# Attention and two expert layers in one kernel: GpSimd's start put in program order, sink rows and second queries on another DMA queue

## The chip, the cores and the metric

One core of a Trainium2 chip. The metric is device time of one execution in microseconds, the median of several runs.

## The reference

Attention over 2 batches, 8 heads, 768 positions and 64 dimensions, with a window of 128 keys and 4 sink keys that every query sees, then two dense layers in a row on the 1536 resulting tokens:

```
keep = is_sink | in_window
scores = np.where(keep, scale * q @ k.T, -1e9)
a = softmax(scores)                       # per query
x = (a @ v) as [1536, 512]
h = x @ moe_w_in;  g = where(h >= 1, h, where(h <= -1, 0, (h + 1)**2 / 4));  x = g @ moe_w_out
h = x @ moe2_w_in; g = where(h > 0, h, exp(min(h, 0)) - 1);                  return g @ moe2_w_out
```

The weights and the two numbers `n_sink` and `window` arrive as 64-bit values and are turned into fp32 on the chip.

## The kernel before

Attention is cut into segments of 256 queries (two blocks of 128); each segment has four jobs, one for a pair of heads. A job has these stages: `st_T` transposes k and q on TensorE into a PSUM bank (`qkps`, L466), copies them to `qkT` (L470) and puts the sink keys beside them: GpSimd copies the first four keys of a batch to `sk` (L480) and `sk` into `qkT` (L481), and keeps the last key block of the segment for the next one (`kept`, L474 and L476). `st_S` makes the scores `S` (L506), VectorE adds the mask and takes the maximum (L510), ScalarE takes the exponential (L512), GpSimd collects the sink columns in `psn` (L515). `st_X` transposes the result (`tps`, L539; copied by ScalarE to `pt`, L541). `st_V` multiplies by v (`ops`, L564). When a segment's four jobs are done, `st_sink` adds the sinks' part: `xps` with the matrix `vs` (L597) and `rps` with the matrix of ones `one` (L601). Its result goes to `xh` and `xl` (L607, L608).

`vs` is built by `vsink` from the sink rows of v, `vraw`. In the first call it also makes two constant sets, `one` and `sel`, with memsets and selects on GpSimd (L362 to L376). `load_vsink` loads `vraw` for both batches on ScalarE's DMA queue (L350); `load` puts the queries of the first two jobs there too (L398) and everything else on SyncE's queue.

The dense layers walk over blocks of 512 tokens and 16 slices of the hidden dimension: `gemm1` makes `h` (L171), `gemm2` adds to `y` (L210), each with three fp32r products of a high and a low part. A weight unit is loaded into `st` (L106, L109; three buffers) and converted from 64-bit by ScalarE (`ca` L138, `F` L139) and VectorE (`ca` L142 and L143, `F` L145), then split into `wh` (L158) and `wl` (L160).

A scheduler sets the order on each engine by priorities, except inside `manual_schedule`, where the named engines (TensorE alone, L766 and L773) keep the program's order. `go` runs attention's stages: 20 of them, then the rest of the first token block, then the others between the steps of the dense layers. DMAs of both queues take eight semaphores in turn, so each waits for the landing of the eighth before it.

Of the kernel before, what the change touches and what calls it, by code (L numbers as in the profile page):

```python
# [7 lines left out]
F32 = mybir.dt.float32  # L8
F32R = mybir.dt.float32r
# [3 lines left out]
ALU = mybir.AluOpType  # L13
# [5 lines left out]
NSINK = 4  # L19
# [262 lines left out]
class Attn:  # L282
# [61 lines left out]

    def load_vsink(self):
        R = self.H * NSINK
        self.vraw, self.vs, self.sel = [], {}, None
        for b in range(self.B):
            raw = self.const.tile([R, 1, self.D], F32, tag=f"vraw{b}", name=f"vraw{b}")
            self.nc.scalar.dma_start(out=raw[:, 0, :], in_=self.v[b, :, 0:NSINK, :])  # L350
            self.vraw.append(raw)

    def vsink(self, b):

        if b in self.vs:
            return self.vs[b]
        nc, const, H, D = self.nc, self.const, self.H, self.D
        R = H * NSINK
        L = 3 * R + 2 * H
        if self.sel is None:  # L360

            self.one = const.tile([L, H, D], F32R, tag="one", name="one")  # L362
            one = const.tile([L, H], F32, tag="oneh", name="oneh")
            nc.gpsimd.memset(one, 0.0)
            for j in range(2):
                nc.gpsimd.affine_select(out=one[3 * R:], in_=one[3 * R:], pattern=[[-1, H]],
                                        compare_op=ALU.not_equal, fill=1.0, base=-j * H, channel_multiplier=1)
            nc.gpsimd.tensor_copy(self.one, one.unsqueeze(2).to_broadcast([L, H, D]))
            self.sel = const.tile([3 * R, H], F32, tag="sel", name="sel")
            nc.gpsimd.memset(self.sel, 1.0)  # L370
            for g in range(3):
                s = self.sel[g * R:(g + 1) * R]
                nc.gpsimd.affine_select(out=s, in_=s, pattern=[[-NSINK, H]], compare_op=ALU.is_ge, fill=0.0,
                                        base=0, channel_multiplier=1)
                nc.gpsimd.affine_select(out=s, in_=s, pattern=[[NSINK, H]], compare_op=ALU.is_ge, fill=0.0,
                                        base=NSINK - 1, channel_multiplier=-1)  # L376
        raw = self.vraw[b]
        part = const.tile([3 * R, 1, D], F32R, tag="vpart", name="vpart")
        nc.gpsimd.tensor_copy(part[0:R], raw)
        nc.gpsimd.tensor_copy(part[R:2 * R], raw)  # L380
        nc.gpsimd.tensor_tensor(out=part[2 * R:], in0=raw, in1=f32(part[0:R]), op=ALU.subtract)
        shape = [3 * R, H, D]
        self.vs[b] = const.tile([L, H, D], F32R, tag="vs", name="vs")
        nc.gpsimd.memset(f32(self.vs[b][3 * R:]), 0.0)
        nc.gpsimd.tensor_tensor(out=self.vs[b][0:3 * R], in0=f32(part).to_broadcast(shape),
                                in1=self.sel.unsqueeze(2).to_broadcast(shape), op=ALU.mult)
        return self.vs[b]

    def load(self, what, seg, pr):
        nc, D, nq = self.nc, self.D, self.nq  # L390
        b, q0 = seg[0], seg[1]
        k0 = max(q0 - 1, 0)
        nk = q0 + nq - k0
        src, r0, n = {"q": (self.q, q0, nq), "k": (self.k, q0, nq), "v": (self.v, k0, nk)}[what]
        t = self.ld_p.tile([128, n, 2, D], F32, tag=what + "n", name=what + "n")
        for j in range(2):

            (nc.scalar if what == "q" and (seg, pr) in self.jobs[:2] else nc.sync).dma_start(  # L398
                out=t[:, :, j, :],
                in_=src[b, 2 * pr + j, r0 * BLK:(r0 + n) * BLK, :].rearrange("(n p) d -> p n d", p=128))  # L400
        self.nat[what, seg, pr] = t
# [54 lines left out]
    def st_T(self, seg, pr, st):  # L456
# [15 lines left out]
            self.kept[pr] = self.const.tile([128, BLK], F32, tag=f"kept{pr}", name=f"kept{pr}")  # L472
        if lead:
            nc.gpsimd.tensor_copy(T[:, 0, 0:BLK], self.kept[pr])  # L474
        if q0 + nq < self.S // BLK:
            nc.gpsimd.tensor_copy(self.kept[pr], T[:, nq, 0:BLK])  # L476
        kT, qT = T[:, 1 - lead:1 + nq], T[:, 1 + nq:, 0:BLK]
        if first:
            self.sk[pr] = self.const.tile([128, 1, NSINK], F32, tag=f"sk{pr}", name=f"sk{pr}")
            nc.gpsimd.tensor_copy(self.sk[pr], kT[:, 0:1, 0:NSINK])  # L480
        nc.gpsimd.tensor_copy(kT[:, :, BLK:], self.sk[pr].to_broadcast([128, nq + lead, NSINK]))  # L481
        st["qk", pr] = qT, kT

    def st_S(self, seg, pr, st, n):
# [221 lines left out]
def attention_moe_moe(ctx, tc, q, k, v, n_sink, window, w_in, w_out, w2_in, w2_out, out):  # L706
# [21 lines left out]
    with ExitStack() as c2:  # L728
# [6 lines left out]
        attn = Attn(tc, c2, q, k, v, xts, idn, const, segs, nq=NQ)  # L735
        moe = Moe(tc, c2, ws, out, xts, (full, full), half)

        attn.load("q", *attn.jobs[1])
        attn.load_vsink()
        warm = const.tile([128, 1], F32, tag="warm", name="warm")  # L740
        nc.scalar.activation(warm, half, AF.Exp)

# [18 lines left out]
        attn.spare = [lambda shape, name, t=t: moe.y_ps.tile(shape, F32, tag=t, name=name) for t in ("y0", "y1", "y2", "y3")]  # L761
        attn.spare += [lambda shape, name: moe.h_ps.tile(shape, F32, tag="h", name=name)] * 2

        for what, j in (("k", 1), ("k", 2), ("q", 2), ("v", 0)):
            attn.load(what, *attn.jobs[j])
        with tc.manual_schedule(engines={mybir.EngineType.PE}):  # L766
            go(n=1)
            moe.load(1)
            attn.load("v", *attn.jobs[1])
            moe.load(3)  # L770
            go(n=19)
        flag = windowed(tc, const, prm)
        with tc.manual_schedule(engines={mybir.EngineType.PE}):  # L773
            go(upto=need[0])
        moe.behind = attn.first
        attn.spare = []
# [56 lines left out]
```

## Time and profile before

| | us |
|---|---|
| median of 3 runs (660.87 to 662.45) | 661.15 |
| the profiled execution | 662.93 |
| its span | 661.2 |
| TensorE busy | 638.8 |
| VectorE busy | 376.2 |
| ScalarE busy | 450.6 |
| GpSimd busy | 267.8 |

Busy time is summed over the whole span; what limits a stage is seen only in that stage's rows. A row of a timeline has start, duration, engine, line, operation, output and input, and in brackets how long the engine idled before it and what ended that.

### The profile page before, as it was taken

To read this page: it belongs to the slowest core of one execution; us is meant where nothing else is said; L and a number is where in the kernel's file an instruction comes from. 1 tells how busy PE (TensorE), PEld (TensorE's weight loads), DVE (VectorE), ACT (ScalarE), POOL (GpSimd) and SP (SyncE) were. 2 spreads that over 40 slices of the span, in tenths; PEclk is the share of its full clock that TensorE was granted. 3 is DMA by queue.
4 is the path that set the end of the run, shared out by engine and by line. 5 is a ranking of instruction groups with operands and counts; after the bars stand their busy time and mean duration, and the time that the engine had idled before them with its cause. 6 is when DMAs were issued, how large, how long until landed. Compare 5 with 4: busy or idle time off the path is not lost.

```text
span 661.2 us, 9257 instructions
## 1 busy us (share of the span) xinstructions
PE 638.8 (97%) x3090; PEld 500.5 (76%) x3090; DVE 376.2 (57%) x742; ACT 450.6 (68%) x913; POOL 267.8 (40%) x310
## 2 busy tenths in 40 slices
PE   5899999999999999999999999999999999999995
PEld 2666767766777767888878888888888888888884
DVE  2899989999435244224987878777432222322221
ACT  2998998997666666557768878776655555555542
POOL 4320113112125334443645655554544444444441
PEclk8998999999999999999999999999999999999999
DMA  6577454764200000000433332321010000100001
GB/s 172 126 186 203 126 170 135 207 198 143 56 13 13 13 0 1 1 0 1 159 118 105 99 105 90 109 93 50 0 64 1 0 1 0 64 0 1 1 0 69
DMA packets 66922, 47.91 MB, mean 72 GB/s; under 512 B 44848, under 2 KB 61232, under 8 KB 66864
## 3 DMA queue, kind: packets, MB, share of 16 engines
q1 hardware_dynamic: 65552, 46.94, 24.6%
q8 instruction: 26, 0.43, 0.3%
q10 hardware_dynamic: 1312, 0.28, 0.2%
q14 instruction: 32, 0.26, 0.1%
HBM read 44.06 MB, written 3.15 MB: 71 GB/s over the span
## 4 chain that ended last, share of the span: by engine, by line
PE 81%; DVE 7%; issue 4%; ACT 4%; DMA 2%; POOL 1%; POOLq 0%; SPq 0%; DVEq 0%; ACTq 0%
PE h L171 36%; PE y L210 35%; PE S L506 4%; PE ops L564 3%; PE tps L539 2%; DVE ca L143 2%; PE qkps L466 1%; DVE F L145 1%; DVE ca L142 1%; DVE wl L160 1%; ACT pt L541 1%; DMA st<-in_moe_w_in_dram 1%; DVE P L510 1%; ACT P L512 1%; PE y L267 1%
## 5 line engine op out<-in xcount | busy, mean ns | idle before, releaser
L160 POOL TENSOR_TENSOR wl<-F,wh 128x512 fp32r<-128x512 f32 x160 | 219.6, 1380 | 229.6 <-ACT wh L158 216.9
L158 ACT CAST wh<-F 128x512 fp32r<-128x512 f32 x192 | 117.5, 618 | 97.1 <-PE h L171 89.4
L171 PE MATMUL h<-xh,wh 128*128 128x512 f32 x384 | 154.3, 402 | 0.5 <-DVE g L180 0.5
L171 PE MATMUL h<-xh,wl 128*128 128x512 f32 x384 | 150.5, 392 | 0.0
L171 PE MATMUL h<-xl,wh 128*128 128x512 f32 x384 | 150.5, 392 | 0.0
L187 ACT CAST gh<-g 128x512 fp32r<-128x512 f32 x96 | 59.7, 621 | 62.1 <-DVE g L184 36.2
L188 DVE TENSOR_TENSOR gl<-g,gh 128x512 fp32r<-128x512 f32 x96 | 68.3, 712 | 49.0 <-ACT gh L187 48.7
L184 DVE SCALAR_TENSOR_TENSOR g<-g,h 128x512 f32<-128x512 f32 x48 | 33.0, 687 | 110.9 <-ACT g L183 110.9
L171 PEld LDWEIGHTS h<-xh,wh 128*128 128x128 f32 x384 | 72.4, 189 | 20.6 <-issue 5.3
L171 PEld LDWEIGHTS h<-xh,wl 128*128 128x128 f32 x384 | 72.3, 188 | 15.3
L171 PEld LDWEIGHTS h<-xl,wh 128*128 128x128 f32 x384 | 72.7, 189 | 14.2 <-DVE xl L608 0.4
L210 PE MATMUL y<-gh,wh 128*128 128x512 f32 x192 | 78.4, 408 | 0.0
L210 PE MATMUL y<-gh,wl 128*128 128x512 f32 x192 | 75.2, 391 | 0.0
L210 PE MATMUL y<-gl,wh 128*128 128x512 f32 x192 | 74.9, 390 | 0.0
L145 DVE CUSTOM_DVE_ANT_0 F<-ca,F 128x1024 uint16<-128x1024 uint16 x64 | 71.5, 1119 | 4.5 <-DVE ca L143 1.8
L210 PE MATMUL y<-wh,gh 128*128 128x512 f32 x184 | 71.6, 389 | 0.0
L210 PE MATMUL y<-wl,gh 128*128 128x512 f32 x184 | 71.6, 389 | 0.0
L210 PE MATMUL y<-wh,gl 128*128 128x512 f32 x184 | 71.6, 389 | 0.0
L180 DVE SCALAR_TENSOR_TENSOR g<-h,g 128x512 f32<-128x512 f32 x48 | 33.0, 687 | 45.2 <-ACT g L179 45.1
L512 ACT ACTIVATE P<-P,nb 128x260 f32<-128x260 f32 (+1 forms) x96 | 46.6, 491 | 15.5 <-DVE nb L510 13.4
L515 POOL COPY psn<-P 128x8 f32<-128x8 f32 x48 | 13.0, 271 | 89.8 <-ACT P L512 81.9
L510 DVE CUSTOM_DVE_ANT_0 P<-S,mask 128x260 f32<-128x260 f32 (+1 forms) x96 | 34.8, 401 | 24.1 <-PE S L506 23.5
(105 smaller groups left out, 912.3 us busy)
## 6 DMA issues: line engine op xcount, KB each, us to landing
st<-in_moe_w_in_dram SPq DMA_DIRECT2D x32, 512.0 KB, 3.9
st<-in_moe_w_out_dram SPq DMA_DIRECT2D x32, 512.0 KB, 3.8
kn<-in_k_dram SPq DMA_DIRECT2D x48, 64.0 KB, 2.3
vn<-in_v_dram SPq DMA_DIRECT2D x32, 96.0 KB, 2.4
out_dram<-o SPq DMA_DIRECT2D x12, 256.0 KB, 2.1
qn<-in_q_dram SPq DMA_DIRECT2D x44, 64.0 KB, 2.4
vn<-in_v_dram SPq DMA_DIRECT2D x16, 64.0 KB, 2.1
qn<-in_q_dram ACTq DMA_DIRECT2D x4, 64.0 KB, 3.0
```

Of the source, the lines that this page charges most:

```text
L145: nc.vector.tensor_tensor(out=r, in0=ai, in1=r, op=ALU.add)
L158: nc.scalar.copy(hi, src)
L160: (nc.vector if i < self.KF else nc.gpsimd).tensor_tensor(out=lo, in0=src, in1=f32(hi), op=ALU.subtract)
L171: nc.tensor.matmul(h, lhsT=w[:, k * 128:(k + 1) * 128], rhs=x[:, k, c0:c0 + n], start=(k == 0 and p == 0), stop=(k == self.KD - 1 and p == 2))
L180: nc.vector.scalar_tensor_tensor(out=g, in0=h, scalar=1.0, in1=g, op0=ALU.max, op1=ALU.min)
L184: nc.vector.scalar_tensor_tensor(out=g, in0=g, scalar=-1.0, in1=h, op0=ALU.add, op1=ALU.max)
L187: ac = nc.scalar.copy(gh, g)
L188: dv = nc.vector.tensor_tensor(out=gl, in0=g, in1=f32(gh), op=ALU.subtract)
L210: nc.tensor.matmul(self.y[c], lhsT=a, rhs=b, start=(first and p == 0), stop=(last and p == 2))
L506: nc.tensor.matmul(S[h], lhsT=qT[hs, n, :], rhs=kT[hs].rearrange("p j k -> p (j k)")[:, j0 * KW:j0 * KW + W], start=True, stop=True)
L510: dv = nc.vector.tensor_tensor_reduce(out=o, in0=S[h], in1=self.mask[ty], op0=ALU.add, op1=ALU.min, scale=-self.scale, scalar=3.0e38, accu ...
L512: ac = nc.scalar.activation(o, o, AF.Exp, bias=nb[:, n, h:h + 1], scale=-1.0, accum_out=sm[:, n, 2 * pr + h:2 * pr + h + 1])
```

## The change

The constant sets move from `vsink` into a function of their own, `sink_sets`, which is called ahead of the first stage. `vraw` is loaded on SyncE's queue, behind the first loads of k, q and v. Of the queries only those of the first job stay on ScalarE's queue; those of the second go on SyncE's, between the second and the third keys. In `st_T` the sink keys are copied before the kept block. GpSimd joins TensorE in the parts whose order is the program's, and `windowed`, which makes the flag for the general path, moves into one such part.

```diff
     def load_vsink(self):
-        self.vraw, self.vs, self.sel = [], {}, None
+        self.vraw, self.vs = [], {}
...
-            self.nc.scalar.dma_start(out=raw[:, 0, :], in_=self.v[b, :, 0:NSINK, :])
+            self.nc.sync.dma_start(out=raw[:, 0, :], in_=self.v[b, :, 0:NSINK, :])
             self.vraw.append(raw)
+
+    def sink_sets(self):
+        nc, const, H, D = self.nc, self.const, self.H, self.D
+        R = H * NSINK
+        L = 3 * R + 2 * H
+        self.one = const.tile([L, H, D], F32R, tag="one", name="one")
+        one = const.tile([L, H], F32, tag="oneh", name="oneh")
+        nc.gpsimd.memset(one, 0.0)
+        for j in range(2):
+            nc.gpsimd.affine_select(out=one[3 * R:], in_=one[3 * R:], pattern=[[-1, H]],
+                                    compare_op=ALU.not_equal, fill=1.0, base=-j * H, channel_multiplier=1)
+        nc.gpsimd.tensor_copy(self.one, one.unsqueeze(2).to_broadcast([L, H, D]))
+        self.sel = const.tile([3 * R, H], F32, tag="sel", name="sel")
+        nc.gpsimd.memset(self.sel, 1.0)
+        for g in range(3):
...
     def vsink(self, b):
-        if self.sel is None:
...
     def load(self, what, seg, pr):
-            (nc.scalar if what == "q" and (seg, pr) in self.jobs[:2] else nc.sync).dma_start(
+            (nc.scalar if what == "q" and (seg, pr) == self.jobs[0] else nc.sync).dma_start(
...
     def st_T(self, seg, pr, st):
             nc.gpsimd.tensor_copy(T[:, 0, 0:BLK], self.kept[pr])
-        if q0 + nq < self.S // BLK:
-            nc.gpsimd.tensor_copy(self.kept[pr], T[:, nq, 0:BLK])
...
         nc.gpsimd.tensor_copy(kT[:, :, BLK:], self.sk[pr].to_broadcast([128, nq + lead, NSINK]))
+        if q0 + nq < self.S // BLK:
+            nc.gpsimd.tensor_copy(self.kept[pr], T[:, nq, 0:BLK])
...
-        attn.load("q", *attn.jobs[1])
-        attn.load_vsink()
         warm = const.tile([128, 1], F32, tag="warm", name="warm")
...
-        for what, j in (("k", 1), ("k", 2), ("q", 2), ("v", 0)):
+        for what, j in (("k", 1), ("q", 1), ("k", 2), ("q", 2), ("v", 0)):
             attn.load(what, *attn.jobs[j])
-        with tc.manual_schedule(engines={mybir.EngineType.PE}):
+        attn.load_vsink()
+        attn.sink_sets()
+        with tc.manual_schedule(engines={mybir.EngineType.PE, mybir.EngineType.Pool}):
...
-        flag = windowed(tc, const, prm)
-        with tc.manual_schedule(engines={mybir.EngineType.PE}):
+            flag = windowed(tc, const, prm)
             go(upto=need[0])
```

How this moves instructions shows at three places. The first is GpSimd's queue from its constant sets to the sink keys of the first job (numbers behind a name tell buffers apart). Before:

```order
L379 CAST vpart<-vraw_134 32x64
L380 CAST vpart<-vraw_134 32x64
L366 AFFINE_SELECT oneh<-oneh 16x8
L373 AFFINE_SELECT sel<-sel 32x8 x3
L384 MEMSET vs 16x512
L366 AFFINE_SELECT oneh<-oneh 16x8
L375 AFFINE_SELECT sel<-sel 32x8 x3
L381 TENSOR_TENSOR vpart<-vraw_134,vpart 32x64
L368 CAST one<-oneh 112x512
L476 COPY kept_195<-qkT 128x128
L480 COPY sk_197<-qkT 128x4
L385 TENSOR_TENSOR vs<-vpart,sel 96x512
```

The same place in the changed kernel:

```order
L361 AFFINE_SELECT oneh<-oneh 16x8
L368 AFFINE_SELECT sel<-sel 32x8 x3
L361 AFFINE_SELECT oneh<-oneh 16x8
L370 AFFINE_SELECT sel<-sel 32x8 x3
L363 CAST one<-oneh 112x512
L481 COPY sk_214<-qkT 128x4
L482 COPY qkT<-sk_214 128x2x4
L484 COPY kept_213<-qkT 128x128
```

The steps on `vraw` and `vs` have left this place; they stand now behind the sink copies (`psn`) of the sixth job.

The second place is SyncE's DMA queue from its start, behind the load of `window`. Before:

```order
L398 DMA kn<-in_k_dram 128x2x64 x6
L398 DMA qn<-in_q_dram 128x2x64 x2
L398 DMA vn<-in_v_dram 128x2x64 x2
L106 DMA st<-in_moe_w_in_dram 128x4x256
L398 DMA vn<-in_v_dram 128x2x64 x2
L398 DMA kn<-in_k_dram 128x2x64 x2
L398 DMA qn<-in_q_dram 128x2x64 x2
L109 DMA st<-in_moe_w_out_dram 128x1024
L106 DMA st<-in_moe_w_in_dram 128x4x256
```

The same queue in the changed kernel:

```order
L401 DMA kn<-in_k_dram 128x2x64 x4
L401 DMA qn<-in_q_dram 128x2x64 x2
L401 DMA kn<-in_k_dram 128x2x64 x2
L401 DMA qn<-in_q_dram 128x2x64 x2
L401 DMA vn<-in_v_dram 128x2x64 x2
L350 DMA vraw_182<-in_v_dram 32x1x64
L350 DMA vraw_184<-in_v_dram 32x1x64
L106 DMA st<-in_moe_w_in_dram 128x4x256
L401 DMA kn<-in_k_dram 128x2x64 x2
L401 DMA qn<-in_q_dram 128x2x64 x2
L401 DMA vn<-in_v_dram 128x2x64 x2
L109 DMA st<-in_moe_w_out_dram 128x1024
```

Two query loads and two loads of `vraw` are new ahead of the first weights `st`; each keys or queries row of two is one job.

The third place is ScalarE from the exponentials of the third job to those of the fourth and the copy (`pt`) behind them. Before:

```order
L512 ACTIVATE P,sm<-P,nb 128x132 x2
L512 ACTIVATE P,sm<-P,nb 128x260 x2
L541 COPY pt<-tps 128x384 x2
L138 ACTIVATE ca<-st 128x512
L139 ACTIVATE F<-st 128x512
L512 ACTIVATE P,sm<-P,nb 128x132 x2
L512 ACTIVATE P,sm<-P,nb 128x260 x2
L541 COPY pt<-tps 128x384 x2
```

The same place in the changed kernel:

```order
L515 ACTIVATE P,sm<-P,nb 128x132 x2
L515 ACTIVATE P,sm<-P,nb 128x260 x2
L544 COPY pt<-tps 128x384 x2
L138 ACTIVATE ca<-st 128x512
L139 ACTIVATE F<-st 128x512
L138 ACTIVATE ca<-st 128x512
L139 ACTIVATE F<-st 128x512 x2
L138 ACTIVATE ca<-st 128x512
L158 CAST wh_926<-F 128x512
L515 ACTIVATE P,sm<-P,nb 128x132 x2
L515 ACTIVATE P,sm<-P,nb 128x260 x2
L544 COPY pt<-tps 128x384 x2
```

The conversions of the second and third weight units and the first `wh` now stand ahead of the fourth job's exponentials.

## Rows read from the trace of the kernel before

**Rows 1.** The page, part 1: busy us (share of the span) xinstructions by engine

```profile
PE 638.8 (97%) x3090; PEld 500.5 (76%) x3090; DVE 376.2 (57%) x742; ACT 450.6 (68%) x913; POOL 267.8 (40%) x310
```

**Rows 2.** Stretches: us, their length, busy us by engine, PE clock, DMA share, GB/s

```profile
10.00:20.00 10.00, 6.21 (x38) 4.21 (x38) 3.74 (x18) 4.18 (x17) 6.03 (x24) 0.66 0.92 244
...
24.00:58.00 34.00, 29.21 (x233) 21.34 (x229) 32.56 (x110) 33.28 (x97) 7.77 (x31) 1.00 0.68 174
...
83.00:110.00 27.00, 26.41 (x142) 19.55 (x137) 24.88 (x57) 24.23 (x54) 8.09 (x14) 1.00 0.54 159
```

**Rows 3.** Chain of waits, 0 to 30 us: start, us, what

```profile
2.01 6.15 issue
...
9.73 0.52 POOL vs L384
...
13.79 1.68 PE S L506 x8
```

**Rows 4.** Timeline of POOL, 0 to 24 us: start, us, instruction, idle before

```profile
8.18 0.23 POOL L379 CAST vpart<-vraw 32x64 fp32r<-32x64 f32 x1 [6.17 <-DMA vraw<-in_v_dram]
...
8.99 0.69 POOL L373 TENSOR_SCALAR_AFFINE_SELECT sel<-sel 32x8 f32<-32x8 f32 x3
...
11.64 0.61 POOL L368 CAST one<-oneh 112x512 fp32r<-112x512 f32 x1
...
12.57 1.03 POOL L385 TENSOR_TENSOR vs<-vpart,sel 96x512 fp32r<-96x512 f32 x1
```

**Rows 5.** Timeline of ACT and its DMA queue (ACTq), 0 to 24 us

```profile
1.28 3.98 ACTq L398 DMA_DIRECT2D qn<-in_q_dram  x4
5.40 2.05 ACTq L350 DMA_DIRECT2D vraw<-in_v_dram  x2
7.49 1.28 ACT L741 ACT_TABLE_LOAD   x1 [7.49 <-DMA qn<-in_q_dram]
...
8.89 1.05 ACT L470 COPY qkT<-qkps 128x512 f32<-128x512 f32 x2
```

**Rows 6.** Timeline of PE, 0 to 24 us

```profile
7.00 0.44 PE L466 MATMUL qkps<-idn,qn 128*128 128x128 f32 x2
...
19.30 0.93 PE L506 MATMUL S<-qkT 64*128 64x132 f32 x8
```

**Rows 7.** SP's DMA queue: timeline to 30 us; waits (us, times, longest)

```profile
8.37 0.47 SPq L106 DMA_DIRECT2D st<-in_moe_w_in_dram  x1
...
11.02 0.93 SPq L398 DMA_DIRECT2D qn<-in_q_dram  x2
...
SPq L398 <- DMA prm_i<-in_window_dram: 1.8, 1, 1.8
```

**Rows 8.** Single DMAs issued at 4.88, 11.48, 13.03, 11.99 us: KB, us to landing

```profile
qn<-in_q_dram ACTq DMA_DIRECT2D x1, 64.0 KB, 2.1
...
qn<-in_q_dram SPq DMA_DIRECT2D x1, 64.0 KB, 2.6
...
kn<-in_k_dram SPq DMA_DIRECT2D x1, 64.0 KB, 5.0
...
st<-in_moe_w_out_dram SPq DMA_DIRECT2D x1, 512.0 KB, 4.2
```

**Rows 9.** Timelines of DVE (first row) and of ACT (second), 0 to 24 us

```profile
7.63 0.50 DVE L343 TENSOR_SCALAR mask<-mask 128x260 f32<-128x260 f32 x2
...
22.95 0.67 ACT L138 ACTIVATE ca<-st 128x512 f32<-128x512 f32 x1
```

**Rows 10.** Timelines of POOL, PE, DVE and PE, 22 to 62 us

```profile
33.79 0.66 POOL L515 COPY psn<-P 128x8 f32<-128x8 f32 x1 [0.55 <-ACT P L512]
...
35.70 0.50 PE L597 MATMUL xps<-pst,vs 112*128 112x256 f32 x2
...
37.66 1.28 DVE L604 TENSOR_TENSOR xb<-xps,xb 128x512 f32<-128x512 f32 x2
...
58.00 0.73 PE L171 MATMUL h<-xh,wh 128*128 128x512 f32 x2
```

More of the change, by code (lines that the diff above doesn't have):

```diff
@@ L346, in load_vsink @@
         R = self.H * NSINK
-        self.vraw, self.vs, self.sel = [], {}, None
+        self.vraw, self.vs = [], {}
         for b in range(self.B):
             raw = self.const.tile([R, 1, self.D], F32, tag=f"vraw{b}", name=f"vraw{b}")
-            self.nc.scalar.dma_start(out=raw[:, 0, :], in_=self.v[b, :, 0:NSINK, :])
+            self.nc.sync.dma_start(out=raw[:, 0, :], in_=self.v[b, :, 0:NSINK, :])
             self.vraw.append(raw)
+    def sink_sets(self):
[12 more added lines that the diff above has]
+        for g in range(3):
+            s = self.sel[g * R:(g + 1) * R]
+            nc.gpsimd.affine_select(out=s, in_=s, pattern=[[-NSINK, H]], compare_op=ALU.is_ge, fill=0.0,
+                                    base=0, channel_multiplier=1)
+            nc.gpsimd.affine_select(out=s, in_=s, pattern=[[NSINK, H]], compare_op=ALU.is_ge, fill=0.0,
+                                    base=NSINK - 1, channel_multiplier=-1)
     def vsink(self, b):
@@ L359, in vsink @@
         L = 3 * R + 2 * H
-        if self.sel is None:
[L362 to L376, printed above, removed]
         raw = self.vraw[b]
```

## The prediction, made before the changed kernel ran

> **What bounds the kernel now.** I read the page first: TensorE (PE) is busy for 97% of the span [rows 1], so a change to GpSimd (POOL) can only pay where PE is not the limit. The table of stretches says where that is. Behind 58 us PE is the limit: from 83 to 110 us it is busy 26.41 of 27 us. From 24 to 58 us ScalarE (ACT) is busy 33.28 of 34 us and VectorE (DVE) 32.56; from 10 to 20 us nobody is the limit: ACT works 4.18 us, DVE 3.74 us, and PE's clock is 0.66 on average [rows 2]. So there are three stages: a start that waits, a stage of attention and weight conversion that ACT and DVE fill, and from the first `h` matmul at 58.00 us [rows 10] a stage that PE fills. What is won at the start counts if it reaches that first `h`.
>
> The chain of waits names the start: 6.15 us from 2.01 us on in which it finds no work, then POOL's steps one by one, then the first score matmuls `S` at 13.79 us [rows 3]. The timeline of POOL shows why. Its first cast of the sink rows waited 6.17 us for the load of `vraw`, and everything behind it in POOL's queue stood still: the selects that make `sel` and `oneh`, `one`, and at the end `sk`, the copy of the sink keys without which no `S` may start [rows 4]. The timeline of ACT shows a second thing: its queue issues four q loads (3.98 us) and two `vraw` loads (2.05 us) before the table load at 7.49 us, so the first `qkT` is copied out of PSUM only at 8.89 us, while PE had finished the transposes of the second job at about 7.44 us [rows 5, 6]. The DMA queue of SyncE (SP) shows a third: each DMA waits for the eighth before it, 1.8 us at the ninth [rows 7].
>
> **The change, part by part.**
>
> *POOL's sets and its order.* The eight selects and `one` no longer stand behind the load. Three selects took 0.69 us, so eight are about 1.9 us, with `one` at 0.61 us [rows 4] 2.5 us: from 2.0 us on they are over by 4.6 us, before any `qkT` exists. Cost nothing; the cover is the wait for k and q. The five steps that build `vs` (two casts of 0.23 us and a product of 1.03 us [rows 4], a memset of 0.52 us [rows 3], a short subtraction: about 2.4 us with the gaps) go behind the sixth job's sink copies.
>
> *ACT's queue.* Two q loads instead of six loads. The four took 3.98 us with a wait among them, so two end between 2.3 and 3.3 us; with 1.28 us of table load and the warming exp ACT is free by 4.8 us at the latest, and the first `qkT` copy (half of 1.05 us) follows PE's transposes, ending at 6.9 us [rows 5]. `sk` and its copy into `qkT` take 0.4 us: ready at 7.3 us.
>
> *The second q on SP.* PE's order puts the transposes of the second job ahead of the first `S`. Its q is now the ninth DMA and waits for the parameter load, as the ninth did at 4.5 us; one that was issued at 4.88 us on ACT landed 2.1 us later [rows 8]. On SP the two go out at 4.9 and 5.4 us, land at 7.0 and 7.5 us, and with 0.44 us of transposes [rows 6] the first `S` starts at about 7.8 us instead of 13.79 us. **Lead: 6.0 us.** DVE then does the last two mask steps (0.50 us [rows 9]) behind the first mask-and-max, where they used to be covered: 0.5 us off.
>
> *SP's queue.* This is where I expect most of the lead to go. Ahead of the fourth k and q now stand the second q (two DMAs) and `vraw` (two) besides what stood there. Two q loads take 0.93 us on SP [rows 7], so k2, q2 and v0 take it from 5.8 to 8.6 us. `vraw` has no row on SP: on ACT the two took 2.05 us [rows 5], while other loads take 0.46 us each, so 0.9 to 2.05 us; I take 2.0, the row of the same load. Then `st` (0.47), k3 and q3: the last q3 DMA goes out at 12.5 us instead of 11.5 us. Before, it landed 2.6 us after issue, and the following k load, beside two weight loads, needed 5.0 us [rows 8]. I take 2.6: landed at 15.1 us. PE's order needs these transposes ahead of the third job's `S`, which so starts at 15.4 us instead of 19.30 us [rows 6]: **lead 3.9 us**, and the 0.5 us of the masks lies inside that wait. By the bounds (`vraw` at 0.46 us each; landing in 5.0 us) the lead is 5.0 or 1.5 us. Less idle could also spare PE the half clock at which its first eight `S` took 1.68 us against 0.93 us later [rows 3, 6]; but PE idles again before q3 lands, so I count nothing.
>
> The Trainium skill ("DMA: Bandwidth & Descriptors", section "Issuing engines are not separate DMA queues") says that issuing from several engines saves only the sequencer's time, usually small against the DMA. ACT's rows differ: there six issues held up the copies until 7.49 us. By the rule `vraw` would cost SP next to nothing, the lead would be 5.0 us and the time about 657.1 us.
>
> *ACT and DVE to the first `h`.* In the new order ACT converts three weight units and casts one `wh` in a row before the exps of the fourth job, where it did one unit. At about 0.6 us a conversion [rows 9] the surplus is some 2.9 us of work done earlier, not added. It starts 3.9 us earlier, at 19.1 us instead of 22.95 us [rows 9]. The third unit's weights are the eighth DMA behind the first unit's and wait for them: out at 10.6 us, landed 4.2 us later [rows 8] at 14.8 us, so the third unit's land at about 19.5 us. They are wanted four conversions behind 19.1 us, at 21.5 us, so I count no wait. Up to the last `xh` of the first token block, ACT's order holds one conversion step more than before (7 `ca` against 6): **0.6 us off**. DVE's holds one `ca` step and one `wl` more; it idles 1.44 us in that stage [rows 2], which takes them.
>
> *`vs` late.* `vs` now starts behind the sink copies of the sixth job, which ended at 34.45 us; 2.4 us later is 36.9 us on before's scale, where the `xps` matmuls ran at 35.70 us [rows 10]. PE would wait up to 1.2 us there; but DVE took the result only at 37.66 us [rows 10], behind other work. So 0 to 1.2 us; I take 0.4: **0.4 us off**.
>
> Everything else (kept keys behind sink keys; the flag inside the hand-ordered part) is off the path.
>
> **Sum.** 3.9 - 0.6 - 0.4 = 2.9 us earlier at the first `h`, 55.1 us instead of 58.00. From there PE has the same matmuls left and hardly idles, so the end moves with it. The profiled span is 661.2 us (that execution took 662.93 us); the median of the runs is 661.15 us. 661.15 - 2.9 = **658.2 us**.
>
> **Rivals.**
>
> 1. *The DMAs don't hold it.* `vraw` costs SP 0.46 us each, q3 lands in time, and ACT and DVE carry 5 to 6 us of lead on: 661.15 - 5.5 = 655.7 us. For it: DMAs of 64 KB landed in 2.1 us when the queue was short [rows 8]. Against it: SP's queue is longer by four DMAs, and the first unit's weights go out at 10.6 us instead of 8.37 us [rows 7].
>
> 2. *SP's queue takes nearly all of it.* q3 needs 5.0 us to land beside the weights: lead 1.5 us, less 1.0 us: 660.6 us, within what the measurement of this kernel can tell from no change (0.3%, 2.0 us: 659.2 to 663.1). For it: the row of 5.0 us [rows 8]. Against: at its issue only one weight load is in flight.
>
> 3. *Slower: ACT stands at the third unit's weights.* ACT works in order, and the exps of the fourth job now stand behind that conversion. The weights are issued only after the first unit's have landed. Until 21.5 us they cost nothing; each us beyond comes off the lead, and with 2.9 us to lose and 2.0 us to be seen it decides from a landing at 26.4 us on, 6.9 us later than I work out. With 27.0 us the time is 661.15 + 5.5 - 2.9 = 663.8 us. For it: SP's queue runs late by four DMAs. Against: two landings of 4.2 us one behind the other [rows 8] leave 2 us to spare.
>
> 4. *It does nothing for the end.* The lead reaches the first `h`, but the new mix of conversions and attention behind it lets PE wait as long: 661 us. For it: PE's order changes from the first `h` on. Against: PE idles 0.6 us in 83 to 110 us [rows 2], so there is little to re-mix, and conversions are further ahead.
>
> **How the numbers follow.** Forecast 0.44, rival 1 0.20, rival 2 0.24, rival 3 0.06, rival 4 0.06. The forecast's own spread is 656.6 to 659.6 us, nearly all of it below 659.2 us. Faster by over 0.3%: 0.41 of the forecast, 0.20 of rival 1 and a little of rival 2: 0.62. Within 0.3%: the rest of the forecast, of rival 2 and rival 4: 0.32. Slower: 0.06. The range goes from rival 1 with some room (655.0) to rival 2 with some room (661.1); what lies outside is rival 3, part of rival 4 and a lead above 6 us, under 0.2 in all.
>
> **What would show it.** In the changed kernel's trace: POOL without a wait for `vraw` ahead of `sk`; the table load before 4 us; first `S` near 7.8 us; third job's `S` near 15.4 us with PE waiting for a q load; conversions of three units in a row on ACT from about 19 us without a DMA wait; first `h` near 55 us; and the same distance from there to the end, 603 us. I am wrong if the third job's `S` does not wait for a DMA (rival 1), if it starts after 17 us (rival 2), if ACT waits on `st` before the fourth job's exps (rival 3), or if the stretch behind the first `h` changes by more than 1.5 us.

## The result and the profile after

The changed kernel takes 667.11 us (median of 5 runs, 665.92 to 668.61); the kernel before takes 661.15 us (660.73 to 662.45, 5 runs beside them). The ratio is 1.0088, with a 95% interval from 1.0067 to 1.0108: **slower by 6.0 us**, where I had forecast 2.9 us faster. The profiled execution of the changed kernel took 668.61 us, at the upper end of its runs; its span is 666.9 us, against 661.2 us before. Executions of one kernel differ here by up to 4.5 us, and the mean granted clock of PE differs between them, too (0.987 in the profiled execution of the changed kernel, 0.992 in the median one), so I take sizes from medians and places from traces.

PE's own work did not grow: it has the same 3090 instructions as in [rows 1], and they take 5.1 us longer.

```profile
PE 643.9 (97%) x3090; PEld 502.1 (75%) x3090; DVE 377.4 (57%) x742; ACT 451.7 (68%) x913; POOL 267.6 (40%) x310
```

The stretches of [rows 2] in the changed kernel (us, length, busy us by engine, PE clock, DMA share, GB/s):

```profile
10.00:20.00 10.00, 7.20 (x41) 4.14 (x40) 5.25 (x26) 6.33 (x26) 2.31 (x14) 0.71 0.84 228
24.00:58.00 34.00, 28.56 (x220) 21.14 (x218) 31.31 (x110) 29.95 (x87) 11.03 (x38) 0.95 0.65 162
83.00:110.00 27.00, 27.00 (x144) 19.38 (x143) 24.65 (x54) 24.63 (x52) 7.28 (x12) 1.00 0.49 146
```

From 24 to 58 us ACT and DVE now idle 4.05 and 2.69 us, where they idled 0.72 and 1.44 us before, and PE's clock is no longer 1.00 throughout. The stage that two engines filled now has holes. The chain of waits names other things at the start than in [rows 3]: the warm-up matmuls instead of GpSimd, and then a k load (start, us, what):

```profile
1.56 5.49 PE warmup L748 x6
11.57 3.55 DMA kn<-in_k_dram
```

PE's timeline shows where the lead goes (start, us, instructions; in brackets the idle time before and what ended it):

```profile
8.89 0.93 PE L509 MATMUL S<-qkT 64*128 64x132 f32 x8 [0.28 <-POOL qkT L482]
15.25 0.66 PE L469 MATMUL qkps<-idn,kn 128*128 128x128 f32 x2 [2.80 <-DMA kn<-in_k_dram]
16.41 1.68 PE L509 MATMUL S<-qkT 64*128 64x132 f32 x8
21.58 0.93 PE L509 MATMUL S<-qkT 64*128 64x132 f32 x8
25.04 0.44 PE L469 MATMUL qkps<-idn,kn 128*128 128x128 f32 x2 [0.92 <-DVE qkT L473]
27.77 1.24 PE L567 MATMUL ops<-pt,vn 128*64 128x256 f32 x8 [0.91 <-ACT pt L544]
34.72 0.59 PE L587 MATMUL sps<-idn,psn 128*48 128x128 f32 x2 [2.59 <-DVE psn L584]
35.10 1.92 PE L542 MATMUL tps<-idn,P 128*128 128x128 f32 x8
39.01 0.51 PE L600 MATMUL xps<-pst,vs 112*128 112x256 f32 x2
60.70 0.73 PE L171 MATMUL h<-xh,wh 128*128 128x512 f32 x2 [0.28 <-ACT xh L610]
```

The same row of `sps` in the kernel before:

```profile
33.00 0.38 PE L584 MATMUL sps<-idn,psn 128*48 128x128 f32 x2 [1.49 <-DVE psn L581]
```

The first `S` is 4.9 us earlier than before, the third job's 2.9 us earlier [rows 6], the fourth job's only 1.0 us (21.58 against 22.62 us). Then the lead turns: the sink transposes `sps` are 1.7 us late, the `xps` matmuls 3.3 us, the first `h` 2.7 us [rows 10].

Two kinds of loss stand in these rows. One is **the clock**: behind the wait of 2.80 us the third job's eight `S` take 1.68 us, where the first eight took 0.93 us. The granted clock is 0.50 there, the 1.2 GHz level, and 0.59 from 34 to 38 us, behind the wait of 2.59 us (stretches, columns as above):

```profile
16.00:20.00 4.00, 4.00 (x21) 2.29 (x21) 2.39 (x10) 1.98 (x8) 0.95 (x6) 0.50 1.04 309
34.00:38.00 4.00, 3.28 (x16) 2.93 (x18) 2.25 (x6) 2.56 (x6) 3.73 (x7) 0.59 0.44 100
```

The other is **the order** on ACT and DVE. ACT's timeline:

```profile
2.30 1.28 ACT L742 ACT_TABLE_LOAD   x1 [2.30 <-issue]
17.69 0.40 ACT L515 ACTIVATE P<-P,nb 128x132 f32<-128x132 f32 x1 [3.04 <-DVE nb L513]
21.50 0.67 ACT L138 ACTIVATE ca<-st 128x512 f32<-128x512 f32 x1
...
24.98 0.60 ACT L158 CAST wh<-F 128x512 fp32r<-128x512 f32 x1
25.49 0.40 ACT L515 ACTIVATE P<-P,nb 128x132 f32<-128x132 f32 x1
```

From 21.50 us on stand six conversion steps and a cast, three units' worth, ahead of the fourth job's exps at 25.49 us. Before, one unit stood there and these exps began at 24.11 us, although the job's `S` came 1.0 us later. DVE's timeline of the same stretch and of the sink chain:

```profile
22.20 0.43 DVE L142 TENSOR_SCALAR ca<-ca 128x512 int32<-128x512 int32 x1 [2.17 <-ACT ca L138]
...
24.90 0.28 DVE L513 CUSTOM_DVE_ANT_0 P<-S,mask 128x132 f32<-128x132 f32 x1
...
33.03 0.24 DVE L582 RECIPROCAL sm<-sm 128x16 f32<-128x16 f32 x1
33.19 0.62 DVE L143 SCALAR_TENSOR_TENSOR ca<-st,ca 128x512 int32<-128x512 int32 x1
33.73 0.16 DVE L583 CAST psn<-sm 128x16 fp32r<-128x16 f32 x1
33.81 0.68 DVE L160 TENSOR_TENSOR wl<-F,wh 128x512 fp32r<-128x512 f32 x1
34.41 0.16 DVE L584 TENSOR_TENSOR psn<-sm,psn 128x16 f32<-128x16 f32 x1
34.49 0.68 DVE L145 CUSTOM_DVE_ANT_0 F<-ca,F 128x1024 uint16<-128x1024 uint16 x1
35.10 0.72 DVE L160 TENSOR_TENSOR wl<-F,wh 128x512 fp32r<-128x512 f32 x1
```

DVE, too, idles 2.17 us and then does four conversion steps, while the `S` of the fourth job, there from 21.58 us on, waits until 24.90 us for its mask-and-max. And a `wl` step of 0.68 us stands inside the sink chain on which PE waits. SP's queue:

```profile
8.88 1.61 SPq L350 DMA_DIRECT2D vraw<-in_v_dram  x2
12.13 0.93 SPq L401 DMA_DIRECT2D qn<-in_q_dram  x2
15.17 0.96 SPq L401 DMA_DIRECT2D kn<-in_k_dram  x2
```

The load issued last here is the fifth job's k. Its two DMAs (KB, us to landing):

```profile
kn<-in_k_dram SPq DMA_DIRECT2D x2, 64.0 KB, 5.0
```

Before, it was issued at 13.03 us and also needed 5.0 us [rows 8]; now it lands 2.1 us later, at 20.2 to 20.7 us, and PE transposes it from 20.82 us on.

GpSimd did what the change says (`one` over at 4.7 us, then free). In the sink chain its casts for `vs` ran slowly:

```profile
4.07 0.61 POOL L363 CAST one<-oneh 112x512 fp32r<-112x512 f32 x1
8.40 0.19 POOL L481 COPY sk<-qkT 128x4 f32<-128x4 f32 x1 [3.71 <-ACT qkT L473]
34.48 0.79 POOL L382 CAST vpart<-vraw 32x64 fp32r<-32x64 f32 x1
35.32 0.58 POOL L383 CAST vpart<-vraw 32x64 fp32r<-32x64 f32 x1
```

The two casts, which took 0.23 us each ([rows 4] shows the first), take 0.79 and 0.58 us here, beside DVE's `F` and `wl` steps. The Trainium skill ("SBUF — State Buffer", section "Summary: rules for kernel authors") says that of a DVE step with two SBUF inputs and a GpSimd step that reads SBUF the second to issue is blocked until the first ends. The second cast agrees: it starts within DVE's `wl` step, which goes from 35.10 to 35.82 us, and ends just behind it, at 35.90 us. For the first cast the rows don't tell which of the two was issued first (34.48 and 34.49 us).

### The profile page after: what moved, and what is told of

Same layout as the page of the kernel before. It is cut to its first block, busy times and chain, and to the rows that moved or that the text cites. A ratio compares the mean times of both kernels' runs of the same rounds, so it can differ in the third digit from the quotient of the medians.

```text
span 666.9 us, 9253 instructions
## 1 busy us (share of the span) xinstructions
PE 643.9 (97%) x3090; PEld 502.1 (75%) x3090; DVE 377.4 (57%) x742; ACT 451.7 (68%) x913; POOL 267.6 (40%) x310
## 4 chain that ended last, share of the span: by engine, by line
PE 81%; ACT 6%; DVE 6%; issue 3%; DMA 2%; POOL 0%; POOLq 0%; SPq 0%; DVEq 0%; ACTq 0%
PE h L171 36%; PE y L210 34%; PE S L509 3%; PE tps L542 2%; PE ops L567 2%; ACT P L515 1%; DVE ca L143 1%; PE qkps L469 1%; DVE ca L142 1%; PE warmup L748 1%; ACT pt L544 1%; ACT ca L138 1%; DMA st<-in_moe_w_out_dram 1%; ACT wh L158 1%; PE y L267 1%
## 5 line engine op out<-in xcount | busy, mean ns | idle before, releaser
L518 POOL COPY psn<-P 128x8 f32<-128x8 f32 x48 | 12.5, 260 | 95.0 <-ACT P L515 87.1
L143 DVE SCALAR_TENSOR_TENSOR ca<-st,ca 128x512 int32<-128x512 int32 x64 | 45.9, 721 | 1.1
```

Source lines behind the costliest of these rows:

```text
L143: nc.vector.scalar_tensor_tensor(out=ai, in0=w1, scalar=-0x80000000, in1=ai, op0=ALU.bitwise_and, op1=ALU.bitwise_or)
```

## The experiments

**Theory at the start**: the lead of the start is real, and it is lost through the order of ACT and DVE, which is not written by hand and came out differently once the loads were moved, and through PE's idling. **Rival A**: SP's longer queue is the loss. **Rival B**: GpSimd's program order is, with `vs` made late. The median of the kernel before was 661.1 to 661.3 us beside all of these runs. The table has the starts of stages on PE in each trace (us) and the median of the runs (us).

| kernel | first S | third S | fourth S | sps | xps | first h | median |
|---|---|---|---|---|---|---|---|
| before | 13.79 | 19.30 | 22.62 | 33.00 | 35.70 | 58.00 | 661.15 |
| after | 8.89 | 16.41 | 21.58 | 34.72 | 39.01 | 60.70 | 667.11 |
| e1 GpSimd part alone | 10.02 | 15.20 | 19.23 | 29.62 | 33.53 | 55.40 | 659.80 |
| e2 moved loads alone | 11.95 | 18.35 | 21.70 | 34.70 | 39.02 | 60.62 | 665.06 |
| e3 after, vraw later on SP | 8.27 | 14.79 | 21.36 | 32.30 | 36.63 | 58.31 | 665.83 |
| e4 after, order held | 8.48 | 16.16 | 21.70 | 31.67 | 36.95 | 59.42 | 665.31 |
| e5 e1, vs early | 10.00 | 15.08 | 19.54 | 29.94 | 32.64 | 56.87 | 660.44 |
| e6 e4, vs early | 8.33 | 16.17 | 22.18 | 31.65 | 35.50 | 56.48 | 662.61 |
| e7 after, wl held | 8.62 | 16.17 | 21.77 | 33.30 | 37.62 | 58.55 | 664.48 |
| e8 after, vs early | 9.01 | 16.75 | 21.94 | 35.06 | 39.30 | 61.02 | 667.84 |
| e9 e6, fifth k first | 8.32 | 16.60 | 21.79 | 32.27 | 36.01 | 57.55 | 662.97 |
| e10 e6, vraw on ACT | 8.58 | 15.14 | 20.24 | 32.08 | 34.77 | 56.28 | 660.80 |
| e11 e1, vraw behind the exp | 8.82 | 14.84 | 19.92 | 31.75 | 35.41 | 56.70 | 660.17 |
| e12 e1, fifth k first | 9.95 | 15.09 | 18.41 | 28.97 | 32.63 | 53.86 | 659.29 |
| e13 e12, vs early | 10.00 | 14.76 | 18.22 | 29.66 | 32.36 | 54.03 | 658.69 |
| e14 e13, vraw behind the exp | 8.83 | 15.07 | 19.03 | 29.73 | 32.42 | 54.12 | 659.02 |

### The two halves of the change

**e1, GpSimd's part alone.** The changed kernel with its loads and flag put back:

```diff
-            (nc.scalar if what == "q" and (seg, pr) == self.jobs[0] else nc.sync).dma_start(
+            (nc.scalar if what == "q" and (seg, pr) in self.jobs[:2] else nc.sync).dma_start(
...
-            self.nc.sync.dma_start(out=raw[:, 0, :], in_=self.v[b, :, 0:NSINK, :])
+            self.nc.scalar.dma_start(out=raw[:, 0, :], in_=self.v[b, :, 0:NSINK, :])
...
+        attn.load("q", *attn.jobs[1])
+        attn.load_vsink()
         warm = const.tile([128, 1], F32, tag="warm", name="warm")
```

> The kernel before with the GpSimd part of the change alone: constant sets first, GpSimd in the program's order, sink keys ahead of kept keys. The second q and vraw stay on ACT's queue, so SP's queue is the old one, and PE's order is that of the kernel before (ACT's and DVE's but for a handful of places). Theory (what costs is the new order of ACT's and DVE's work that came with the moved loads, and PE's idling; GpSimd's part is good): first S at about 10.3 us instead of 13.79 (ACT is still held by its six issues until its table load at 7.49 us), 3 us of it reach the first h, 657 to 659 us. Rival A (the moved loads alone, by the longer SP queue): the same 657 to 659 us. Rival B (GpSimd's program order is what costs: vs is made late, and its steps are slow beside DVE): first h no earlier than 58.0, 661 to 665 us.

659.80 us (657.41 to 660.40), ratio 0.9970 (0.9957 to 0.9982): **faster**, though 0.8 us above the range of the theory, and rival B falls. The trace shows the wait for `vs` that I had put at 0.4 us:

```profile
10.02 0.94 PE L509 MATMUL S<-qkT 64*128 64x132 f32 x8 [2.70 <-POOL qkT L482]
33.53 0.51 PE L600 MATMUL xps<-pst,vs 112*128 112x256 f32 x2 [1.14 <-POOL vs L388]
```

**e2, the moved loads alone**, on the kernel before (the same lines the other way round; GpSimd as before).

> The kernel before with the moved loads alone (second q and vraw on SP); GpSimd as before, so that it still waits for vraw ahead of the sink copies. Theory: ACT and DVE get the new order (three units converted in a row behind the third job's exps) and the first S comes only with vraw at 12 to 13 us: 664 to 669 us, slower than before. Rival A: SP's queue costs the same here: 664 to 669 us. Rival B: without GpSimd's order there is no loss: 658 to 662 us.

665.06 us (662.50 to 665.42), ratio 1.0043 (1.0027 to 1.0059): **slower**, as expected. ACT's instructions stand in the changed kernel's order up to 42.9 us, and PE has its waits, so the new order came with the loads, not with GpSimd's part:

```profile
25.55 0.44 PE L466 MATMUL qkps<-idn,kn 128*128 128x128 f32 x2 [1.31 <-DVE qkT L470]
28.29 1.23 PE L564 MATMUL ops<-pt,vn 128*64 128x256 f32 x8 [0.91 <-ACT pt L541]
34.70 0.38 PE L584 MATMUL sps<-idn,psn 128*48 128x128 f32 x2 [2.05 <-DVE psn L581]
```

**e3, the same order with another queue**: on SP the two `vraw` loads go behind the fourth k and q.

```diff
-        attn.load_vsink()
         attn.sink_sets()
...
             attn.load("v", *attn.jobs[1])
+            attn.load_vsink()
             moe.load(3)
```

> The changed kernel with the two vraw loads moved on SP behind the first weight load, the fourth k and q and the second v. The order of PE, ACT, DVE and GpSimd is that of the changed kernel, only SP's differs: the last q DMA that PE waits for goes out about 1.6 us earlier. Theory (order, not queue): that wait shrinks from 2.8 to about 1.2 us, 0.5 to 1 us of it is left at the first h, 665.5 to 667 us. Rival A (SP's longer queue and the wait on it are the cause): 658 to 662 us. Rival B: no change, 667 us.

665.83 us (663.48 to 667.76), ratio 1.0075 (1.0062 to 1.0089): 1.3 us less than the changed kernel, as the theory said, but the two intervals overlap, so that rival B isn't excluded. (Its profiled execution was the fastest of its runs.) The fourth k now lands in time for a third `S` at 14.79 us, but the fourth `S` comes at 21.36 us, hardly earlier than in the changed kernel: `vraw` still stands ahead of the fifth k. Behind the fourth `S` this trace loses little, although its order is the changed kernel's on PE, ACT, DVE and GpSimd. ACT's timeline has the same conversions, begun 2.4 us earlier:

```profile
19.11 0.67 ACT L138 ACTIVATE ca<-st 128x512 f32<-128x512 f32 x1
23.08 0.41 ACT L515 ACTIVATE P<-P,nb 128x132 f32<-128x132 f32 x1
```

The fourth job's exps follow 1.72 us behind its `S`, against 3.91 us in the changed kernel, and `sps` 10.9 us behind it, against 13.1 us (10.4 us before). So, by these two traces, what this order costs depends on how late the third job is when ACT comes to the conversions.

### The order

**e4, order held.** The second to fourth conversion each stand behind the exps of one job more, and the first two `wl` steps behind `psn`:

```diff
-        if n == nq - 1 and (seg, pr) == self.jobs[2]:
-            self.first = (ac.ins, dv.ins)
+        if n == nq - 1 and (seg, pr) in self.jobs[2:7]:
+            self.first = (self.first or []) + [(ac.ins, dv.ins)]
...
-        after = self.behind if self.n_cv <= 4 else self.own ...
+        after = self.behind and self.behind[(0, 1, 2, 2)[self.n_cv - 1]] if self.n_cv <= 4 else self.own ...
...
+        with self.tc.issue_after(self.psn) if self.psn and i < 2 else nullcontext():
-        (nc.vector if i < self.KF else nc.gpsimd).tensor_tensor(out=lo, ...
+            (nc.vector if i < self.KF else nc.gpsimd).tensor_tensor(out=lo, ...
```

> The changed kernel with the order held: the second, third and fourth weight conversion each stand behind the exps of one attention job more (fourth, fifth, fifth job instead of all behind the third), and the first two wl steps behind the two psn steps of DVE. Loads and GpSimd as in the changed kernel. Theory: the lead of the start (4.9 us at the first S, 2.9 us at the third job's) stays, first h at 55.5 to 57.5 us, 658 to 661 us. Rival A (queue): the wait for the fourth q is still there, 665 to 668 us. Rival B (GpSimd's order): 665 to 668 us.

665.31 us (664.10 to 665.86), ratio 1.0055 (1.0042 to 1.0068): a miss for the theory, inside the range of both rivals. `sps` did move 3.1 us forward, to 31.67 us, but the next thing was late, `vs` on GpSimd, whose product ended at 36.90 us (the profile names `nb`, which was done long before):

```profile
36.95 0.80 PE L603 MATMUL xps<-pst,vs 112*128 112x256 f32 x2 [2.49 <-DVE nb L514]
```

**e6, order held and vs early**: GpSimd builds `vs` between the third and the fourth job.

```diff
-            go(n=19)
+            go(n=6)
+            attn.vsink(0)
+            go(n=13)
```

> The changed kernel with the order of conversions and of wl held, and vs built earlier on GpSimd as well. With the order held alone PE waited 2.49 us at the first xps matmuls until vs was there at 36.9 us, and ran the next 3 us at half clock. Theory: with vs early the wait is bounded by pst (35.4 us), no half clock behind it, first h 1.5 to 2.5 us earlier than with the order held alone, 662 to 664 us. Rival (the moved loads cost whatever the order): 665 us as before.

662.61 us (660.95 to 663.48), ratio 1.0018 (1.0009 to 1.0027): as expected. **e8** is the control, `vs` early without the order held.

> The changed kernel with vs built earlier on GpSimd, nothing else; the order of PE, ACT, DVE and SP is that of the changed kernel. In the changed kernel vs was there at 37.94 us and the xps matmuls ran at 39.01 us behind the score matmuls. Theory (there the sink chain of DVE and the half clock are the limit, not vs): 666.5 to 667.5 us, no change. Rival (GpSimd's late vs is the loss): 661 to 665 us.

667.84 us (665.75 to 668.14): 0.3 us above the range, but no change, as expected. In the changed kernel `vs` was late behind something later still. So holding the order is worth 667.84 - 662.61 = 5.2 us where `vs` is early, and 667.11 - 665.31 = 1.8 us where it is not (there the two intervals touch). In the traces of e8 and e6 4.5 us of the 5.2 us are there at the first `h` (61.02 against 56.48 us); behind it the two also differ in PE's order.

**e7, wl alone held**: only the last two lines of the diff of e4.

> The changed kernel with one order alone mended: the first two wl steps of DVE stand behind the two psn steps of the first segment. ACT's order is that of the changed kernel; conversions are still pulled forward. Theory: the sink transposes sps start 0.6 to 0.7 us earlier than in the changed kernel, and the sum is 665.5 to 667 us: the greater part of the loss is in the conversions and at the start. Rival (the wl step in the sink chain and the half clock behind it are the whole loss): 661 to 664 us.

664.48 us (663.62 to 666.50): 2.6 us less, more than I expected. In the trace `sps` comes 1.4 us earlier, but 1.0 us of that is there already at the sixth job's `S` (29.22 against 30.18 us), through a shorter half clock at the start, and 0.4 us is the `wl` step. Behind `sps` PE loses less to the clock, 0.8 us more, so that the seventh job's `S` is 2.2 us earlier (35.62 against 37.80 us). So some 1.2 us are the step's own in this trace; whether the rest of the 2.6 us is scatter, or comes from ACT's order behind 42 us, which came out differently with this edit, too, stays open. The whole loss it isn't.

### The loads

**e9**: e6 with the fifth k and q ahead of two weight loads on SP, and **e12**: the same on e1.

```diff
-            moe.load(3)
-            go(n=6)
+            go(n=1)
+            moe.load(3)
+            go(n=5)
```

> The changed kernel with the order held and vs early, as in the run before that gave 662.61 us, and one thing more: on SP the fifth job's k and q are issued ahead of the second and third weight load instead of behind them. PE's order stays, ACT's and DVE's change in a few places. Theory now (two causes: the order, which is held here, and SP's queue, which makes PE wait for the fifth k): the fifth k goes out at 14.1 us instead of 15.2 and not beside two weight loads, lands at 17 to 18 us instead of 21.2, the fourth job's S starts at 19.5 to 20.8 us instead of 22.18, and 1 to 2 us of it stay: 660.5 to 661.7 us. Rival A (the queue costs nothing, the order was all): 662.6 us. Rival B (weights are wanted as soon as they land): the conversions wait for st, 662.6 to 664 us.

662.97 us (661.00 to 665.52): a miss, nothing won. PE no longer waits for the fifth k, but waits 3.54 us for the fourth and then runs at half clock until 21 us, so that the fourth `S` comes at 21.79 us all the same.

> The kernel of the GpSimd part alone (659.8 us), with the fifth job's k and q issued ahead of the second and third weight load on SP. PE's order is that of the runs with the order held. Theory (the fifth k bounds the start): fourth job's S 0.5 to 1 us earlier than the 19.23 us of that kernel, 658.5 to 660 us. Rival (the weights, landed 2 us later, hold up the conversions): 660.5 to 662 us.

659.29 us (658.05 to 660.09), ratio 0.9966 (0.9953 to 0.9979): as expected, fourth `S` at 18.41 us. PE's order in e9 and e12 is the same, so this pair pointed to the loads themselves, apart from the order (but `vs` is early in e9 alone).

**e10**: e6 with `vraw` back on ACT, but behind its table load and warming exp (the call `attn.load_vsink()` one line below `warm`, on `nc.scalar`).

> The changed kernel with the order held and vs early, and with the two vraw loads issued by ACT again, but behind its table load and warming exp, so that they hold up no copy; the second q stays on SP. SP's queue is 1.6 us shorter ahead of the fourth and fifth k. Theory (order and SP's queue): fourth k landed at about 13.6 us instead of 15.2, fifth at about 19.6 us instead of 21.2, fourth job's S at about 20.5 us instead of 22.18, 660.5 to 661.7 us. Rival A (order alone): 662.6 us. Rival B (the 2 us of ACT's issues hold up the first copies): first S at 9.5 us or later instead of 8.33, 662 to 664 us.

660.80 us (659.26 to 662.29), ratio 0.9994 (0.9984 to 1.0005): 1.8 us less than e6, as expected, fourth `S` at 20.24 us. There the lead on e6 is 1.94 us, near the 1.61 us that the two loads took on SP. But the 1.8 us can't be put to the loads alone: the order of ACT and DVE changed with them from 21 us on and PE's from 65 us on, and at the first `h` only 0.20 us of the lead are left in the traces. Behind it e6 ran in part at half clock and e10 did not (granted clock 0.87 and 1.00 from 55 to 68 us).

**e13** has the old loads with PE's order, the early `vs` and the late weights of e9: the loads alone, at one order of PE and GpSimd (places on ACT and DVE differ, all of them behind the fourth `S`).

> The GpSimd part with the fifth k and q ahead of the second and third weight load (659.29 us), and vs early as well. Order of PE is that of the changed kernel with order held, vs early and the same weights late (662.97 us), ACT's and DVE's but for a few places; what differs is the loads: second q and vraw here on ACT, there on SP. Theory (the moved loads cost by themselves, through the 3.5 us that PE waits for the fourth k and the half clock behind it): 658 to 659.5 us, so that the loads alone are worth 3.5 to 5 us at one order. Rival (the loads cost only through the order): 661.5 to 663 us. The 0.90 us that PE waited for vs goes, or turns into a wait for pst.

658.69 us (658.13 to 660.01), ratio 0.9961 (0.9948 to 0.9975): as expected, 4.3 us less than e9. First e9's timeline of PE and its stretch from 16 to 20 us (columns as above):

```profile
15.36 0.66 PE L470 MATMUL qkps<-idn,kn 128*128 128x128 f32 x2 [3.54 <-DMA kn<-in_k_dram]
16.60 1.68 PE L510 MATMUL S<-qkT 64*128 64x132 f32 x8
21.79 0.93 PE L510 MATMUL S<-qkT 64*128 64x132 f32 x8
```

```profile
16.00:20.00 4.00, 4.00 (x21) 2.29 (x21) 2.19 (x10) 1.98 (x8) 1.51 (x8) 0.50 0.80 218
```

The same two views of e13:

```profile
13.98 0.41 PE L469 MATMUL qkps<-idn,kn 128*128 128x128 f32 x2 [0.51 <-DVE nb L513]
14.76 0.93 PE L509 MATMUL S<-qkT 64*128 64x132 f32 x8
18.22 0.93 PE L509 MATMUL S<-qkT 64*128 64x132 f32 x8 [0.38 <-POOL qkT L482]
```

```profile
16.00:20.00 4.00, 3.62 (x35) 2.55 (x32) 2.91 (x15) 4.00 (x15) 3.68 (x14) 1.00 1.08 312
```

In these 4 us PE has 21 matmuls in e9 and 35 in e13. The fourth `S` is 3.57 us apart, the first `h` 3.52 us, the medians 4.28 us. The 3.57 us are there before any instruction of these engines stands in another place.

### What bounds the start

**e11**, e1 with `vraw` behind the warming exp, and **e14**, e13 with the same:

> The kernel of the GpSimd part alone (659.8 us), with the two vraw loads moved on ACT behind the table load and the warming exp. Order and SP's queue stay those of that kernel. Theory (the fifth k, landed at about 18.3 us, bounds the start there): first S at 8.2 to 8.8 us instead of 10.02, but the fourth job's S again at about 19.0 us, and the time 659.3 to 660.3 us. Rival (what the first S wins goes through to the end): 658.0 to 658.8 us.

660.17 us (658.90 to 661.47).

> As the run before in this call, with the two vraw loads on ACT behind its table load and warming exp: first S at about 8.7 us instead of 9.95. Theory (the fourth k, landed at about 14 us, bounds the start, and a PE that comes earlier waits for it): fourth job's S within 0.5 us of the run without, the time the same within 0.6 us. Rival (the first S decides): 1 us less.

659.02 us (658.02 to 660.34). Both as expected in the time: a first `S` that is 1.2 us earlier changes nothing that can be measured. PE comes earlier and waits for the fourth k (1.75 and 1.70 us). In e11 it then waits 1.72 us for the fifth k as well, and the fourth `S` is 0.7 us later than in e1. In e14 the wait for the fourth k is followed by 0.83 of the clock from 16 to 20 us, and the fourth `S` is 0.8 us later than in e13, more than the 0.5 us I had allowed.

**e5**, e1 with `vs` early:

> The kernel of the GpSimd part alone, with vs of the first batch built earlier in GpSimd's program order (between the third and the fourth job, where GpSimd idles) instead of behind the sink copies of the sixth. The order of PE, ACT, DVE and SP stays. There PE waited 1.14 us for vs ahead of the first xps matmuls. Theory: this wait was the price of vs made late and falls away, first h 0.5 to 1.1 us earlier, 658.3 to 659.3 us against 659.8 us. Rival: pst or the banks are late next, no gain, 659.8 us.

660.44 us (657.75 to 661.84), nothing won: a miss. `xps` came 0.9 us earlier, but ACT then waited 1.36 us for a weight load (0.55 us in e1), PE 1.92 us for ACT's copy (1.34 us in e1), and what followed ran at half clock:

```profile
43.29 2.19 PE L567 MATMUL ops<-pt,vn 128*64 128x128 f32 x12 [1.92 <-ACT pt L544]
```

## Why the prediction was wrong

**GpSimd's sets: right.** They are over at 4.7 us, and `sk` waits for ACT's copy, not for `vraw`.

**ACT's queue and the first S: right in kind, 1.1 us short.** The table load comes at 2.30 us instead of 7.49 us. In this execution the warm-up matmuls took 5.49 us and put off the first transposes to 6.84 us (5.69 us in e9); first `S` at 8.89 us instead of the 7.8 us predicted. e11 and e14 show that, with the old loads, it doesn't matter.

**SP's queue: right to the fourth k, and then broken off.** `vraw` took 1.61 us (I took 2.0), the two q loads of the fourth job went out from 12.13 us on (I said 12.5 for the last), and the fourth k landed at 15.1 us (11.57 + 3.55), the time I gave for q. By my working the third `S` would have followed at 15.4 us; PE began the transposes ahead of it at 15.25 us, and at half clock they took until 16.41 us. The step that failed is "PE idles again before q3 lands, so I count nothing": the new wait has a price of its own, the half clock behind it, and I looked only at what the old idling might give back. And I stopped at the fourth k. The fifth job's k stands behind two weight loads and moved by the same 2.1 us, so that from there on the start was worth 1.0 us, not 3.9 us. The rule of the Trainium skill that I weighed there ("DMA: Bandwidth & Descriptors", section "Issuing engines are not separate DMA queues": a change of issuing engine saves only sequencer time, usually small) holds here in that what moved was time of the queue, but that time was not small: without the two `vraw` loads of 1.61 us on SP the fourth `S` came 1.94 us earlier (e6 to e10), and the whole move cost 4.3 us at one order of PE (e9 to e13).

**ACT and DVE to the first h: this step decided.** I wrote of the surplus of conversions, 2.9 us, that it is "work done earlier, not added", gave it no price, took off 0.6 us for one more step alone, and wrote that DVE's idle time "takes" its extra `ca` and `wl`. Work that is not added still costs where it stands ahead of something that PE waits for: ahead of the fourth job's exps, and between two `psn` steps. I had it start at 19.1 us. The third job was late, by PE's wait and the half clock behind it, so it started at 21.50 us, 1.45 us ahead of the 22.95 us before; so the exps behind it came 1.4 us later than before, not earlier (25.49 against 24.11 us). In e3, with this order and a start at 19.11 us, they came 1.0 us earlier than before. Between the fourth `S` and `sps` the changed kernel loses 2.8 us, at `sps` and behind it to `xps` another 1.6 us. With the loads as they are in the changed kernel the order is worth 5.2 us (e8 to e6). An idle sum over 34 us said nothing on a chain of 1.4 us inside them.

**vs late: right in the changed kernel by luck.** It cost nothing there (e8), because the sink chain was later still. Where the chain was earlier PE waited for it, 1.14 us in e1 and 2.49 us in e4, the upper end of my bounds or beyond. What that wait was worth differs: without it e6 is 2.7 us faster than e4, and e5 no faster than e1.

**First h to the end: wrong, by a smaller sum.** I forecast 603 us; it was 606.2 us. To PE's last matmul it is 599.2 us instead of 597.0 us; 0.8 us lie behind the last matmul of this execution. That the 2.2 us belong to the order isn't shown: with the changed kernel's order on PE, ACT and DVE this stretch takes 598.4 us in e8 and 596.7 us in e3, and with the order held 598.1 us in e6. The clock sets e3 apart (granted clock 1.00 from 56 to 68 us, 0.86 in e8 and e6), but not the changed kernel from the one before (0.86 in both). PE's waits behind the first `h`, up to 155 us (waits, us, times, longest), sum up to 1.5 us, against 1.0 us before:

```profile
PE tps L542 <- DVE nb L513: 0.9, 1, 0.9
PE S L509 <- ACT pt L544: 0.6, 2, 0.5
```

What makes up the 2.2 us stays open.

**The rivals.** Rival 1 falls (the third `S` waited for a DMA). Rival 2 saw a true half: SP's queue takes the lead, though by the fifth k and the clock, and its sign, a third `S` behind 17 us, did not show (16.41 us). Rival 3 had the right sign and the wrong mechanism: ACT never waited for the third unit's weights; the exps stood behind conversions whose weights were there. Rival 4 held in that the stretch behind the first `h` changed, but for the worse. The range missed since every case in it took the order of ACT and DVE for free.

**The account.** From the GpSimd part (659.80 us) to the changed kernel (667.11 us) are 7.3 us that the moved loads cost, the place of the flag included. Of these 4.5 us go when the order is held and `vs` is early (to 662.61 us). The 2.8 us that are left are a remainder and not the price of SP's queue: ACT's and DVE's order in e6 is not that of e1, and at one order of PE the loads were worth 4.3 us (e9 to e13). Two causes are shown, the order (e8 to e6) and the loads with the clock behind their waits (e9 to e13). They need not add up: by the traces of e3 and the changed kernel the order costs little where the third job is early. Against the kernel before, GpSimd's part alone gives 1.5 us, and with the fifth k ahead of the weights and `vs` early 2.5 us (e13): that version beats both kernels. The swap of sink and kept keys and the place of the flag were not tried alone.

## What to carry to other kernels

Where a scheduler sets the order of some engines, moving a load can move their work, too: go through what now stands ahead of each instruction that another engine waits for, and price it there, whether it was added or only done earlier. Work drawn forward is free only if it starts as early as you think: give the time at which it starts, and what becomes of it if that slips. Follow a queue that you lengthen to its last user in the stage, not to the first. And a wait that you put in the place of another costs what the clock does behind it as well.

## What the runs showed of the hardware

Waits of PE were followed by rows at the 1.2 GHz level here: 1.68 us instead of 0.93 us for the same eight `S` behind 2.80 us of idling (after) and behind 3.54 us (e9), and in e14 already behind 1.70 us; in e1 the 1.70 us of idling ahead of `sps` were not followed by it, nor in e13 the 2.64 us ahead of the first `S` (0.93 us for the eight, granted clock 1.00 from 8 to 68 us). Two `vraw` loads of 8 KB each took the issuing queue 1.61 us on SP and 2.05 us on ACT [rows 5], where two loads of 64 KB took 0.93 us.
